# Linear attention and a SiLU block on one core: batch 1's exps of q placed further apart, PSUM bank sets in a cycle of four, and a third of one cast moved to GpSimd

## The chip, the cores and the metric

One core of a Trainium2 chip. The metric is the device time of one execution in microseconds (us). The kernel was already tuned; the question is what one more rearrangement of its first 45 us does to the time. Some words used below: PSUM is the memory that TensorE writes its products to; the kernel uses it as eight banks, and a bank is drained when the other engines have read it, so that TensorE may write it again. A transfer is issued when an engine starts it, and lands when its data are there.

## The reference

```python
# q, k, v: 8 batches, 8 heads, 576 positions, 64 columns, float32
q_s = exp(q - max(q)) / sum(...)          # softmax along the 64 columns
k_s = exp(k - max(k)) / sum(...)          # softmax along the 576 positions
kv  = einsum('bhsd,bhde->...', k_s, v)    # 64 x 64 per head
x   = einsum('bhsd,bhde->bhse', q_s, kv)  # 4608 rows of 512 after reordering
h   = x @ w_in                            # 512 -> 2048
out = (h * sigmoid(h)) @ w_out            # 2048 -> 512, float32
```

## The kernel before

The rows run in chunks. Only the opening matters here: batch 0's attention, the first product (w_in) of its 576 rows in 16 column blocks, the second product (w_out), and, between them, batch 1's attention. The start of the opening, with cuts:

```python
WIDE = (4, 0, 2, 6) * 3 + (4, 2, 0, 6)      # first PSUM bank of each of the 16 column blocks

def wide_mm(fb, cs):                        # first product, column block fb, parts cs of the 512 rows of w_in
    for n in range(2):
        for c in cs:
            nc.tensor.matmul(out=PS[:, WIDE[fb] + n, 0:S // 2], ...)

# the queue of loads on GpSimd, in this order
load_w1(0, 4, 0, 2); load_w1(0, 4, 2, 4)    # w_in, first quarter, in two halves
load_w1(4, 8); load_w1(8, 12); load_w1(12, 16)
load(1, "qt", q, 0, nc.gpsimd); load(1, "qt", q, 1, nc.gpsimd)      # q of batch 1
load_w2(0, 4)                               # w_out, first quarter
load(1, "kt", k, 0, nc.gpsimd); load(1, "kt", k, 1, nc.gpsimd)
load_w2(4, 8)
load(1, "vt", v, 0, nc.gpsimd); load(1, "vt", v, 1, nc.gpsimd)      # v of batch 1
...
vcast(0, 1, nc.scalar, 0, 1)                # v of batch 0, second cast: half each
vcast(0, 1, nc.vector, 1, 2)
...
wide_mm(0, (0, 1)); wide_mm(1, (0, 1)); wide_mm(2, (0, 1))          # needs the first half of w_in's first quarter alone
...
def wide(fb):                               # a unit for each column block
    wide_mm(fb, range(2 if fb < 3 else 0, NC))
    wide_silu(fb)                           # tanh on ScalarE, product on VectorE: this frees the banks
...
# placed before unit n; units 0 to 15 are the column blocks, b1 = 16 is the second product's first
plan(9,  lambda: (load_w2(8, 12), exp_q(1, 0, 0, 1)))
plan(10, lambda: (exp_q(1, 0, 1, 2), qsum_pair(1, 0)))              # GpSimd adds halves and quarters
plan(12, lambda: (exp_q(1, 1, 0, 1), qsum_end(1, 0)))
plan(13, lambda: (exp_q(1, 1, 1, 2), qsum_pair(1, 1), qnorm(1, 0, nc.gpsimd)))
plan(b1, lambda: (qsum_end(1, 1), qnorm(1, 1, nc.vector)))
plan(b1 + 6, lambda: ws_op(4, 1))           # a sum of w_in blocks, on VectorE
plan(b1 + 7, lambda: kv_both(1))            # kv product of batch 1, then its copy on VectorE
plan(b1 + 8, lambda: xt(1, 0))              # first product with that kv matrix
```

The softmax here doesn't subtract the row's maximum and nothing guards it: scores larger than these inputs give would overflow.

Of the kernel before, what the change touches and what calls it, by code (L numbers as in the profile page):

```python
# [17 lines left out]
def kernel(  # L18
# [9 lines left out]
    nc = tc.nc  # L28
    B, H, S, D = q.shape
# [3 lines left out]
    J = S // P  # L33
    NG = H // 2
    NC = DM // 128
# [31 lines left out]
    vaug = glob.tile([128, J, NG, E1], BF16, name="vaug")  # L67
# [19 lines left out]
    def copy(eng, o, i):  # L87
        if eng is nc.scalar:
            eng.copy(out=o, in_=i)  # L89
        else:  # L90
            eng.tensor_copy(o, i)  # L91

    def load(b, name, src, cc, eng):
        t = ld.tile([128, 2, J * D], FP32, name=name)
        st[b][name, cc] = t
        x = src[b].rearrange("(g r) (p j) d -> g (r p) (j d)", r=2, j=J)
        eng.dma_start(out=t, in_=x.rearrange("g x y -> x g y")[:, 2 * cc:2 * cc + 2, :])

    def jgd(b, name, cc):
        return st[b][name, cc].rearrange("p g (j d) -> p j g d", d=D)  # L100

    def half(t, cc):
        return t[:, :, cc * 128:(cc + 1) * 128].rearrange("p j (g d) -> p j g d", d=D)

    def exp_q(b, cc, g0=0, g1=2):
        if "eq" not in st[b]:
            st[b]["eq"] = ap.tile([128, J, NG * D], BF16, name="eq")
        nc.scalar.activation(  # L108
            out=half(st[b]["eq"], cc)[:, :, g0:g1], in_=jgd(b, "qt", cc)[:, :, g0:g1], func=ACT.Exp
        )  # L110

    def exp_k(b, cc):
        nc.scalar.activation(out=half(ek, cc), in_=jgd(b, "kt", cc), func=ACT.Exp)  # L113

    def vcast(b, cc, eng, g0=0, g1=2):
        o = vaug[:, :, 2 * cc + g0:2 * cc + g1, 0:D]
        i = jgd(b, "vt", cc)[:, :, g0:g1, :]
        copy(eng, o, i)

    def vcast_at(t, b, cc):  # L120

        if t == 2 and cc == 1:
            nc.gpsimd.tensor_copy(gate, SS[2][0:1, 0, 0:1])
        vcast(b, cc, nc.gpsimd)

    def qsum_pair(b, cc):
        e = half(st[b]["eq"], cc)
        t1 = mp.tile([128, 2 * TCH], FP32, name="h0", bufs=1)[:, 0:J * D]
        t1 = t1.rearrange("p (j g d) -> p j g d", g=2, d=D // 2)
        t2 = mp.tile([128, 2 * TCH], FP32, name=f"h{cc + 1}", bufs=1)[:, 0:J * D // 2]  # L130
        t2 = t2.rearrange("p (j g d) -> p j g d", g=2, d=D // 4)
        nc.gpsimd.tensor_tensor(
            out=t1, in0=e[:, :, :, 0:D // 2], in1=e[:, :, :, D // 2:D], op=ALU.add
        )
        nc.gpsimd.tensor_tensor(
            out=t2, in0=t1[:, :, :, 0:D // 4], in1=t1[:, :, :, D // 4:D // 2], op=ALU.add
        )
        st[b]["t2", cc] = t2

    def qsum_end(b, cc):  # L140
        new_zq(b)
        nc.vector.reduce_sum(out=st[b]["zq"][:, cc], in_=st[b]["t2", cc], axis=AX.X)
        nc.vector.reciprocal(out=st[b]["rzq"][:, cc], in_=st[b]["zq"][:, cc])

    def new_zq(b):
        if "zq" not in st[b]:
            st[b]["zq"] = ap.tile([128, 2, J, 2], FP32, name="zq", bufs=2)
            st[b]["rzq"] = ap.tile([128, 2, J, 2], FP32, name="rzq", bufs=2)

    def qsum(b, cc, gs=None):  # L150
        new_zq(b)
        z, e = st[b]["zq"][:, cc], half(st[b]["eq"], cc)
        if gs is None:
            nc.vector.reduce_sum(out=z, in_=e, axis=AX.X)  # L154
        else:
            nc.vector.reduce_sum(out=z[:, :, gs], in_=e[:, :, gs, :], axis=AX.X)
        if gs != 0:
            nc.vector.reciprocal(out=st[b]["rzq"][:, cc], in_=z)  # L158

    def qnorm(b, cc, eng):  # L160
        e = half(st[b]["eq"], cc)
        r = st[b]["rzq"][:, cc]
        eng.tensor_tensor(  # L163
            out=e, in0=e, in1=r[:, :, :, None].to_broadcast([128, J, 2, D]), op=ALU.mult
        )
# [21 lines left out]
    def trcopy(b, cc, j0, j1, bank, eng=nc.vector):  # L187
        t = PS[:, bank, :].bitcast(BF16)[:, 0:(j1 - j0) * 128].rearrange("x (j y) -> x j y", y=128)
        copy(eng, new_qt(b)[:, j0:j1, cc, :], t)
# [50 lines left out]
    def xt_evac(t, cc, bank, d0, d1, o0, eng):  # L240
        o = XTS[t % 2][:, 2 * cc:2 * cc + 2, o0:o0 + d1 - d0]
        copy(eng, o, PS[:, bank:bank + 2, d0:d1])
# [8 lines left out]
    def silu(t, fb, i, o, w):  # L251
        sg = mp.tile([128, S], FP32, name="sg", bufs=3)
        s = sg[:, 0:w]
        if len(i.shape) == 3:
            s = s.rearrange("p (a n) -> p a n", a=2)
        nc.scalar.activation(out=s, in_=i, func=ACT.Tanh, scale=OS)
        nc.vector.scalar_tensor_tensor(  # L257
            out=o, in0=s, scalar=1.0, in1=i, op0=ALU.add, op1=ALU.mult
        )


    WIDE = (4, 0, 2, 6) * 3 + (4, 2, 0, 6)

    def wide_mm(fb, cs):
        for n in range(2):
            for c in cs:
                nc.tensor.matmul(  # L267
                    out=PS[:, WIDE[fb] + n, 0:S // 2],
                    lhsT=W1[:, c, fb * 128:(fb + 1) * 128],
                    rhs=XTS[0][:, c, n * (S // 2):(n + 1) * (S // 2)],  # L270
                    start=(c == 0),
                    stop=(c == NC - 1),
                )

    def wide_silu(fb):
        bank = WIDE[fb]
        silu(
            0, fb, PS[:, bank:bank + 2, 0:S // 2],
            GTS[0][:, fb, :].rearrange("p (a n) -> p a n", a=2), S,
        )  # L280
# [268 lines left out]
    def heat(n, bank=5):  # L549
        for _ in range(n):  # L550
            nc.tensor.matmul(out=PS[:, bank, :], lhsT=warm[:, 0:128], rhs=warm, start=True, stop=True)

    def load_w1(f0, f1, c0=0, c1=NC):
        nc.gpsimd.dma_start(
            out=W1[:, c0:c1, f0 * 128:f1 * 128],
            in_=w_in[c0 * 128:c1 * 128, f0 * 128:f1 * 128].rearrange("(c p) f -> p c f", p=128),
        )

    def load_w2(f0, f1):
        nc.gpsimd.dma_start(  # L560
            out=W2[:, f0:f1, :],
            in_=w_out[f0 * 128:f1 * 128, :].rearrange("(fc p) o -> p fc o", p=128),
        )
# [8 lines left out]
    load_w1(4, 8)  # L572
    load_w1(8, 12)
    load_w1(12, 16)
    load(1, "qt", q, 0, nc.gpsimd)
    load(1, "qt", q, 1, nc.gpsimd)
    load_w2(0, 4)
# [11 lines left out]
    heat(7)  # L589
    qnorm(0, 1, nc.vector)  # L590
    vcast(0, 0, nc.scalar)
    trcopy(0, 0, 0, 5, 0, nc.scalar)
    trcopy(0, 0, 5, J, 1)
# [5 lines left out]
    xt_mm(0, 0, 0, 320, 4, 0)  # L599
    xt_mm(0, 0, 320, 256, 0, 0)  # L600
    heat(3, 6)
    vcast(0, 1, nc.scalar, 0, 1)
    vcast(0, 1, nc.vector, 1, 2)
    trcopy(0, 1, 0, 5, 2, nc.scalar)
    trcopy(0, 1, 5, J, 3)
    kv(0, 1)
# [6 lines left out]
    wide_mm(0, (0, 1))  # L613
    xt_evac(0, 1, 6, 0, 320, 0, nc.scalar)
    xt_evac(0, 1, 2, 0, 256, 320, nc.vector)
    wide_mm(1, (0, 1))
    wide_mm(2, (0, 1))


# [3 lines left out]
    def plan(u, f):  # L623
        at.setdefault(u, []).append(f)

    def wide(fb):
        wide_mm(fb, range(2 if fb < 3 else 0, NC))
        wide_silu(fb)

    for fb in range(NFB):  # L630
        units.append(lambda fb=fb: wide(fb))
# [138 lines left out]

    b1 = begin[1]

    plan(9, lambda: (load_w2(8, 12), exp_q(1, 0, 0, 1)))
    plan(10, lambda: (exp_q(1, 0, 1, 2), qsum_pair(1, 0)))
    plan(12, lambda: (exp_q(1, 1, 0, 1), qsum_end(1, 0)))
    plan(13, lambda: (exp_q(1, 1, 1, 2), qsum_pair(1, 1), qnorm(1, 0, nc.gpsimd)))
    plan(14, lambda: (load(2, "qt", q, 0, nc.gpsimd), load(2, "qt", q, 1, nc.gpsimd)))
    plan(b1 + 2, lambda: (exp_k(1, 0), exp_k(1, 1)))
    plan(b1 + 4, lambda: (tr(1, 0, 0, 5, 6), tr(1, 0, 5, J, 7)))
    plan(b1 + 4, lambda: (trcopy(1, 0, 0, 5, 6, nc.scalar), trcopy(1, 0, 5, J, 7)))  # L780
    plan(b1, lambda: (qsum_end(1, 1), qnorm(1, 1, nc.vector)))
    plan(b1, lambda: load_w2(12, 16))
    plan(b1 + 8, lambda: nc.scalar.copy(out=GTS[1][:, :, 0:64], in_=GTS[0][:, :, TCH:S]))
    plan(b1 + 3, lambda: (load(2, "kt", k, 0, nc.gpsimd), load(2, "kt", k, 1, nc.gpsimd)))
# [76 lines left out]
```

## Time and profile before

| | before |
|---|---|
| median, lowest, highest of three runs | 261.32, 261.06, 261.46 us |
| profiled execution, span | 262.14 us, 260.3 us |
| TensorE, VectorE, ScalarE, GpSimd busy | 97%, 80%, 72%, 25% |
| TensorE's one long idle time between 15 and 45 us | 0.78 us at 28.2 |

The prediction shows the lines of this profile that the forecast rests on.

```profile
24.30 0.65 ACT L256 ACTIVATE sg<-PS 128x576 f32<-128x576 f32 x1 [0.33 <-PE PS L267]
25.79 0.68 ACT L108 ACTIVATE eq<-qt 128x576 bf16<-128x576 f32 x1 [0.84 <-DMA qt<-in_q_dram]
26.38 0.63 ACT L256 ACTIVATE sg<-PS 128x576 f32<-128x576 f32 x1
26.91 0.67 ACT L108 ACTIVATE eq<-qt 128x576 bf16<-128x576 f32 x1
27.48 1.18 ACT L256 ACTIVATE sg<-PS 128x576 f32<-128x576 f32 x2
```

The tanh of block 9 had its input at 25.28, but the exp in front of it in ScalarE's order waited until q landed at 25.77. A size is given to the bank wait of TensorE at 28.96 in two ways: 0.78 us is idle time after the matmul before, and 0.95 us is how much later than due the held matmul started (matmuls in a row start 0.1225 us apart).

### The profile page before, as it was taken

To read this page: it belongs to the slowest core of one execution; us is meant where nothing else is said; L and a number is where in the kernel's file an instruction comes from. 1 tells how busy PE (TensorE), PEld (TensorE's weight loads), DVE (VectorE), ACT (ScalarE), POOL (GpSimd) and SP (SyncE) were. 2 spreads that over 40 slices of the span, in tenths; PEclk is the share of its full clock that TensorE was granted. 3 is DMA by queue.
4 is the path that set the end of the run, shared out by engine and by line. 5 is a ranking of instruction groups with operands and counts; after the bars stand their busy time and mean duration, and the time that the engine had idled before them with its cause. 6 is when DMAs were issued, how large, how long until landed. Compare 5 with 4: busy or idle time off the path is not lost.

```text
span 260.3 us, 6411 instructions
## 1 busy us (share of the span) xinstructions
PE 251.3 (97%) x2732; PEld 203.4 (78%) x2732; DVE 208.0 (80%) x268; ACT 187.5 (72%) x212; POOL 65.8 (25%) x63
## 2 busy tenths in 40 slices
PE   8799899999999999999999999999999999999992
PEld 3467656656888888888888888888888888888881
DVE  2867797998997999799979997999798548855932
ACT  5765978998993899489948995799573848484610
POOL 1743791650460306030603060306000000000003
PEclk9999999999999999999999999999999999999999
DMA  6999999679999585956694869530433003300624
GB/s 247 335 196 297 302 320 330 260 159 393 271 343 230 140 246 191 232 128 170 268 249 112 229 216 213 139 83 3 91 81 83 3 0 82 81 3 1 140 64 121
DMA packets 35964, 45.89 MB, mean 176 GB/s; under 512 B 16208, under 2 KB 21008, under 8 KB 35936
## 3 DMA queue, kind: packets, MB, share of 16 engines
q1 hardware_dynamic: 29568, 33.69, 47.5%
q0 software_dynamic: 6128, 11.60, 17.3%
q8 instruction: 21, 0.34, 0.6%
q10 hardware_dynamic: 240, 0.20, 0.2%
q14 instruction: 7, 0.06, 0.1%
HBM read 36.70 MB, written 9.44 MB: 177 GB/s over the span
## 4 chain that ended last, share of the span: by engine, by line
PE 66%; DVE 3%; POOL 1%; issue 0%; ACT 0%; POOLq 0%; DVEq 0%; ACTq 0%
PE PS L477 34%; PE PS L377 30%; PE PS L234 2%; DVE h L355 1%; PE PS L195 1%; DVE GT L451 1%; POOL out_dram L740 1%; DVE zq L154 0%; DVE ow L725 0%; ACT sc L493 0%; DVE ow L497 0%; DVE rzq L158 0%; POOLq L856 0%; DVE kvn L208 0%; DVE rz L206 0%
## 5 line engine op out<-in xcount | busy, mean ns | idle before, releaser
L355 DVE TENSOR_TENSOR h<-PS,h 128x1024 f32<-128x1024 f32 (+1 forms) x45 | 54.0, 1199 | 12.7 <-ACT h L89 6.3
L477 PEld LDWEIGHTS <-GT 128*128 128x128 f16 x512 | 49.6, 98 | 6.9 <-issue 1.2
L377 PEld LDWEIGHTS <-WS 128*128 128x128 f16 x480 | 46.8, 98 | 6.2 <-issue 0.5
L477 PE MATMUL PS<-W,GT 128*128 128x256 f16 x384 | 49.1, 273 | 0.0
L377 PE MATMUL PS<-XS,WS 128*128 128x256 f16 (+1 forms) x360 | 46.3, 272 | 0.1
L361 ACT ACTIVATE GT<-h 128x1024 f16<-128x1024 f32 (+1 forms) x45 | 46.1, 1047 | 0.1
L89 ACT COPY h<-PS 128x1024 f32<-128x1024 f32 (+1 forms) x35 | 35.1, 1003 | 13.1 <-PE PS L377 12.6
L163 POOL TENSOR_TENSOR eq<-eq,rzq 128x1152 bf16<-128x1152 bf16 x13 | 27.7, 2133 | 53.7 <-DVE rzq L158 53.3
L477 PEld LDWEIGHTS <-S 128*128 128x128 f16 x384 | 37.2, 98 | 5.2 <-issue 1.0
L377 PEld LDWEIGHTS <-W 128*128 128x128 f16 x360 | 34.7, 98 | 4.7 <-issue 0.2
L477 PE MATMUL PS<-T,S 128*128 128x256 f16 x256 | 32.7, 273 | 0.0
L377 PE MATMUL PS<-XT,W 128*128 128x256 f16 (+1 forms) x240 | 29.5, 272 | 0.0
L361 ACT ACTIVATE GT<-PS 128x1024 f16<-128x1024 f32 (+1 forms) x15 | 15.2, 1016 | 18.9 <-PE PS L377 18.9
L91 POOL CAST vaug<-vt 128x1152 bf16<-128x1152 f32 x12 | 14.8, 1240 | 44.4 <-DMA vt<-in_v_dram 36.0
L108 ACT ACTIVATE eq<-qt 128x1152 bf16<-128x1152 f32 (+1 forms) x18 | 19.1, 1059 | 3.3 <-DMA qt<-in_q_dram 3.2
L740 POOL DMA_DIRECT2D out_dram<-ow x5 | 2.7, 547 | 72.3 <-DVE ow L725 72.3
L113 ACT ACTIVATE ek<-kt 128x1152 bf16<-128x1152 f32 x16 | 18.4, 1153 | 1.4 <-DMA kt<-in_k_dram 1.4
L154 DVE TENSOR_REDUCE zq<-eq 128x18 f32<-128x1152 bf16 x12 | 16.1, 1345 | 3.8 <-ACT eq L108 3.8
L267 PE MATMUL PS<-XT,W 128*128 128x288 f16 x128 | 16.2, 286 | 0.8 <-DVE GT L257 0.8
L477 PE MATMUL PS<-W,S 128*128 128x256 f16 x128 | 16.5, 273 | 0.0
L497 DVE SCALAR_TENSOR_TENSOR ow<-PS,sc 128x512 f32<-128x512 f32 x7 | 4.8, 692 | 14.4 <-ACT sc L493 14.4
L267 PEld LDWEIGHTS <-W 128*128 128x128 f16 x128 | 12.4, 98 | 4.6 <-issue 1.2
(79 smaller groups left out, 346.7 us busy)
## 6 DMA issues: line engine op xcount, KB each, us to landing
out_dram<-ow SPq DMA_DIRECT2D x64, 128.0 KB, 2.4
qt<-in_q_dram SPq DMA_DIRECT2D x12, 576.0 KB, 4.7
kt<-in_k_dram SPq DMA_DIRECT2D x12, 576.0 KB, 5.6
vt<-in_v_dram SPq DMA_DIRECT2D x12, 576.0 KB, 5.4
qt<-in_q_dram POOLq DMA_DIRECT2D x4, 576.0 KB, 10.8
kt<-in_k_dram POOLq DMA_DIRECT2D x4, 576.0 KB, 13.8
vt<-in_v_dram POOLq DMA_DIRECT2D x4, 576.0 KB, 12.9
W<-in_moe_w_out_dram POOLq DMA_DIRECT2D x4, 512.0 KB, 15.2
```

The source lines that it names most:

```text
L89: eng.copy(out=o, in_=i)
L91: eng.tensor_copy(o, i)
L108: nc.scalar.activation(out=half(st[b]["eq"], cc)[:, :, g0:g1], in_=jgd(b, "qt", cc)[:, :, g0:g1], func=ACT.Exp)
L113: nc.scalar.activation(out=half(ek, cc), in_=jgd(b, "kt", cc), func=ACT.Exp)
L154: nc.vector.reduce_sum(out=z, in_=e, axis=AX.X)
L163: eng.tensor_tensor(out=e, in0=e, in1=r[:, :, :, None].to_broadcast([128, J, 2, D]), op=ALU.mult)
L267: nc.tensor.matmul(out=PS[:, WIDE[fb] + n, 0:S // 2], lhsT=W1[:, c, fb * 128:(fb + 1) * 128], rhs=XTS[0][:, c, n * (S // 2):(n + 1) * (S / ...
L355: nc.vector.tensor_tensor(out=four(t, i), in0=group_bank(t, True), in1=four(t, i), op=ALU.add)
L361: nc.scalar.activation(out=group_out(t, f, n), in_=x, func=ACT.Silu, scale=1.0 / XS)
L377: nc.tensor.matmul(out=PS[:, bank + p // 2, (p % 2) * HT:(p % 2) * HT + width(t)], lhsT=a[:, c, p * 128:(p + 1) * 128], rhs=bb[:, c, 0:wid ...
L477: nc.tensor.matmul(out=PS[:, bank, m * HN:(m + 1) * HN], lhsT=a[:, fc, m * 128:(m + 1) * 128], rhs=bb[:, fc, :], start=(first and fc == 0) ...
L740: eng.dma_start(out=rows(last, th * HT + a * 128 + i * P)[:, n * HN:(n + 1) * HN], in_=o[i * P:(i + 1) * P, :],)
```

## The change

Intent: place the exps of batch 1's q one at a time between tanhs, so that no bank is drained late; give every column block the bank set of the block four back (before, block 13 took that of block 10); and shorten batch 0's second cast of v by a third on GpSimd. GpSimd's additions for the second half of q's sums go, and VectorE sums that half itself.

```diff
+    def vcast(b, cc, eng, g0=0, g1=2, j0=0, j1=J):        # part of the rows
...
-    WIDE = (4, 0, 2, 6) * 3 + (4, 2, 0, 6)
+    WIDE = (4, 2, 0, 6) * 4
...
     load_w1(12, 16)
+    vcast(0, 1, nc.gpsimd, 0, 2, 6, J)
     load(1, "qt", q, 0, nc.gpsimd)
...
-    vcast(0, 1, nc.scalar, 0, 1)
-    vcast(0, 1, nc.vector, 1, 2)
+    vcast(0, 1, nc.scalar, 0, 1, 0, 6)
+    vcast(0, 1, nc.vector, 1, 2, 0, 6)
...
-    wide_mm(1, (0, 1))
     wide_mm(2, (0, 1))
...
-        wide_mm(fb, range(2 if fb < 3 else 0, NC))
+        wide_mm(fb, range(2 if fb in (0, 2) else 0, NC))
...
-    plan(9, lambda: (load_w2(8, 12), exp_q(1, 0, 0, 1)))
-    plan(10, lambda: (exp_q(1, 0, 1, 2), qsum_pair(1, 0)))
-    plan(12, lambda: (exp_q(1, 1, 0, 1), qsum_end(1, 0)))
-    plan(13, lambda: (exp_q(1, 1, 1, 2), qsum_pair(1, 1), qnorm(1, 0, nc.gpsimd)))
-    plan(14, lambda: (load(2, "qt", q, 0, nc.gpsimd), load(2, "qt", q, 1, nc.gpsimd)))
+    plan(9, lambda: load_w2(8, 12))
+    plan(10, lambda: exp_q(1, 0, 0, 1))
+    plan(11, lambda: (exp_q(1, 0, 1, 2), qsum_pair(1, 0)))
+    plan(14, lambda: (exp_q(1, 1, 0, 1), qsum_end(1, 0), qnorm(1, 0, nc.gpsimd)))
+    plan(15, lambda: qsum(1, 1, 0))
...
-    plan(b1, lambda: (qsum_end(1, 1), qnorm(1, 1, nc.vector)))
+    plan(b1, lambda: (exp_q(1, 1, 1, 2), qsum(1, 1, 1), qnorm(1, 1, nc.vector)))
+    plan(b1, lambda: (load(2, "qt", q, 0, nc.gpsimd), load(2, "qt", q, 1, nc.gpsimd)))
```

More of the change, by code (lines that the diff above doesn't have):

```diff
@@ L113, in exp_k @@
         nc.scalar.activation(out=half(ek, cc), in_=jgd(b, "kt", cc), func=ACT.Exp)
-    def vcast(b, cc, eng, g0=0, g1=2):
-        o = vaug[:, :, 2 * cc + g0:2 * cc + g1, 0:D]
-        i = jgd(b, "vt", cc)[:, :, g0:g1, :]
+    def vcast(b, cc, eng, g0=0, g1=2, j0=0, j1=J):
+        o = vaug[:, j0:j1, 2 * cc + g0:2 * cc + g1, 0:D]
+        i = jgd(b, "vt", cc)[:, j0:j1, g0:g1, :]
         copy(eng, o, i)
```

## The prediction

> **What bounds the kernel now.** I read the page's busy times and slices first, then the times of stretches, then the timeline of the first 45 us (the change touches nothing later), last the issues of single transfers with their time to landing. Page, busy row and slices of 6.5 us:
>
> ```profile
> PE 251.3 (97%) x2732; PEld 203.4 (78%) x2732; DVE 208.0 (80%) x268; ACT 187.5 (72%) x212; POOL 65.8 (25%) x63
> ...
> PE   8799899999999999999999999999999999999992
> ...
> DMA  6999999679999585956694869530433003300624
> ```
>
> TensorE is full, but so are the DMA engines in the first slices. The stretches (window and length, busy PE, PEld, DVE, ACT, POOL, clock, DMA share, GB/s):
>
> ```profile
> 15.00:19.20 4.20, 4.17 (x41) 3.06 (x33) 2.21 (x4) 2.43 (x5) 1.25 (x2) 1.00 1.23 205
> 19.20:28.20 9.00, 8.98 (x72) 7.04 (x73) 6.04 (x10) 6.31 (x11) 3.49 (x5) 1.00 1.17 290
> 28.20:29.00 0.80, 0.04 (x1) 0.04 (x1) 0.80 (x2) 0.80 (x2) 0.75 (x1) 1.00 1.03 373
> 29.00:32.00 3.00, 3.00 (x25) 2.37 (x25) 2.68 (x6) 2.54 (x5) 2.23 (x3) 1.00 1.12 310
> 32.00:39.07 7.07, 7.07 (x47) 3.58 (x45) 6.67 (x11) 5.41 (x7) 7.05 (x8) 1.00 1.14 314
> ```
>
> See the 0.8 us hole in TensorE at 28.2, and a DMA share above 1 in every row: the loads run back to back whatever TensorE does. The timeline (start, length, engine, instruction, idle before it and who ended that):
>
> ```profile
> 15.06 13.12 PE L267 MATMUL PS<-XT,W 128*128 128x288 f16 x104
> ...
> 19.18 8.81 PEld L267 LDWEIGHTS <-W 128*128 128x128 f16 x73 [0.34 <-DMA W<-in_moe_w_in_dram]
> ...
> 28.96 3.10 PE L267 MATMUL PS<-XT,W 128*128 128x288 f16 x24 [0.78 <-DVE GT L257]
> ...
> 31.94 3.61 PE L414 MATMUL PS<-W,GT 128*128 128x512 f16 x16
> ...
> 37.25 1.89 PE L414 MATMUL PS<-W,GT 128*128 128x512 f16 x8
> ...
> 38.28 0.68 ACT L89 CAST vaug<-vt 128x576 bf16<-128x576 f32 x1 [0.30 <-DMA vt<-in_v_dram]
> 38.28 0.76 DVE L91 CAST vaug<-vt 128x576 bf16<-128x576 f32 x1
> ...
> 39.07 0.69 PEld L195 LDWEIGHTS <-ek 64*64 64x64 bf16 x72 [0.42 <-ACT vaug L89]
> 39.07 0.81 PE L195 MATMUL PS<-vaug,ek 64*64 64x65 bf16 x72
> ```
>
> TensorE is held three times. At 19.18 the second quarter of w_in has only just landed. At 28.96 it waits for a PSUM bank that VectorE has not drained; this is the wait that the change aims at. At 39.07 the kv product of batch 1 waits for v's second cast, which both engines began when the transfer landed. Two issues of transfers with KB and us to landing:
>
> ```profile
> 24.93 0.72 POOL L97 DMA_DIRECT2D vt<-in_v_dram  x1 [2.26 <-DVE GT L257]
> ...
> vt<-in_v_dram POOLq DMA_DIRECT2D x1, 576.0 KB, 13.3
> W<-in_moe_w_out_dram POOLq DMA_DIRECT2D x1, 512.0 KB, 15.8
> ```
>
> v's last half is issued at 24.93 and lands 13.3 us later, at 38.2: it stands in a queue. The second row was issued at 19.43 (rows 4 to 7 of w_out's 16 blocks) and lands at 35.2. In the same way the first quarter of w_in lands at 14.2 and 16.05 (two halves), its second quarter at 19.14, its third at 21.7, its last at 24.3, q of batch 1 at 25.77 and 27.2, the first w_out quarter at 29.9, k at 31.4 and 32.9, v's first half at 36.8, the third w_out quarter at 40.7.
>
> **What the Trainium skill says.** "DMA: Bandwidth & Descriptors", section "Issuing engines are not separate DMA queues": all issues end on the same 16 DMA engines, and where one issues from saves only issue time. The trace agrees: landings follow each other by 1.47 us for 589,824 bytes, 401 GB/s, just under the 436 GB/s of its section "Where 436 GB/s comes from". "SBUF — State Buffer", section "Who interferes with whom": a VectorE instruction with two SBUF inputs contends with a GpSimd instruction that reads SBUF. The trace agrees: VectorE's normalisation of q took 1.36 us alone and 1.71 us where it overlapped GpSimd's at 34.2. "Perfetto Trace Analysis", section "Identifying Dependency Chains", has one look up the semaphores waited on; the issued order shows that the kv product now also waits for GpSimd at its 25th matmul.
>
> **The change, part by part.** *Banks.* Before, column block 13 of the first product takes the bank set of block 10, three blocks back; after, every block takes that of four back. Two matmuls cost 2 x 0.1225 us of spacing, a block of eight 0.98 us. A block's set is free some 1.65 us after its matmuls (block 4: ready 20.17, tanh at 20.38, VectorE's product 21.06 to 21.82), so three blocks of 0.98 between leave 1.29 us for delays. The delay before was two exps of 0.68 us in a row with tanhs: block 10's product ran at 28.15 to 28.91, and block 13 started at 28.96 in place of 28.01. That is 0.95 us, and it goes: with exps after tanh 9, 10, 13 and 15 I get the product of block 9 done at 26.7 (needed 28.0), of 10 at 27.8 (needed 29.0), of 11 at 28.9 (needed 30.0).
>
> *The early part.* The cast of 576 elements takes 0.68 us on ScalarE and 0.76 on VectorE; from 1152 in 1.17 and 576 in 0.68 a ScalarE element costs 0.85 ns, so 384 cost 0.16 us less, and VectorE at 1.04 ns 0.20 less. GpSimd's part is 384 elements; its casts of 1152 take 1.24 us, and with the 0.2 us of its one-element copy as a floor, 0.55 us. It starts at 12.83, is done at 13.4, and is read at the 25th of 36 matmuls, near 13.6. The product moves from 13.53 to 13.33, the first column block from 15.06 to 14.87. But then eight matmuls in place of twelve are done before w_in's second half is needed: at 15.85, and it lands at 16.05. Blocks 0 to 3 then end at 16.09 + 24 x 0.1225 = 19.03, and the second quarter lands at 19.14. Block 4 starts at 19.19, as before. The early part gives nothing.
>
> *After block 4.* 96 matmuls at 0.1225 end at 30.95, so the second product starts there in place of 31.94: 0.98 us ahead (0.95 and some spacing). Sixteen of its matmuls at 0.215 reach 34.39; nine transposes (0.5) 34.9; the next block needs w_out's second quarter, landed at 35.27: 0.4 us lost. 0.86 of matmuls to 36.2, transposes 36.7, eight matmuls to 38.4. Then kv waits for v: landed 38.26, cast by 39.04, start 39.07. The last 0.65 us are lost there. Sum of what reaches the end: 0.98 - 0.4 - 0.6 = 0, with at most 0.1 left (TensorE idled 0.09 us before kv in the kernel before).
>
> *Sums of q.* The second half's two GpSimd additions (1.29 and 0.80 us) and VectorE's short reduce (0.45) become two reduces of 0.744 on VectorE. By the order of instructions I get the normalisation's start at 34.29 against 34.23, without GpSimd's beside it, so 0.3 us shorter. VectorE must be free for v's cast at 38.26; before it was at 38.2, now near 37.9 to 38.2. No delay, but little slack.
>
> *GpSimd's queue.* The cast puts about 1 us into the issues of q, w_out and k: 12.34 becomes 13.3. They land 12 to 16 us after their issue, behind w_in, so no landing moves. q of batch 2 is issued earlier (33.5 for 34.67) and also stands in the queue.
>
> **Rivals.** First, the bank wait is on the path to the end and its 0.98 us are kept: 260.35 us. For it: TensorE is 97% busy and its order is unchanged. Against: kv's cast began 0.02 us after a landing, and landings do not depend on TensorE. It would need v to land earlier. Second, a new wait: VectorE late for v's cast by the added 1.04 us of reduces, or GpSimd's cast late and holding the first kv product, or issues late enough to empty the queue: 0.2 to 0.5 us more, 261.6. Against: slack of 0.25 us before w_in's half, 10 us of backlog in the queue. Third, TensorE's earlier work shifts later stages by freeing engines: ScalarE and VectorE work after 39 us hangs on kv, so it moves with it; at most 0.2 us either way.
>
> **Range and chances.** From the gate at 39.07 on, the two programs are the same instructions with the same inputs. I predict 261.2 us: 261.32 less 0.1 at most. The three runs spread over 0.4 us; the first rival gives the low end, 260.5 with part of it kept, the second the high end, 261.7. Two per cent is 5.2 us, over five times the largest effect found: within 0.98, faster 0.01, slower 0.01.
>
> **What would show it.** Right: the 0.78 us wait for VectorE gone and the second product starting near 31.0; block 4 still near 19.2 after a wait for w_in; new waits of about 0.4 us for w_out near 34.9 and 0.6 us for v's cast before kv; kv at 39.0 to 39.1. Wrong: kv before 38.7 (v landed earlier), or after 39.3 with VectorE busy at 38.3 (the reduces are on the path), or equal to before up to 45 us and different later.

## The result, and the profile after

| | before | after |
|---|---|---|
| median, lowest, highest of four runs | 261.39, 261.06, 261.50 us | 261.56, 261.29, 261.79 us |
| ratio, 95% interval | | 1.0008 (0.9991 to 1.0026) |
| profiled execution, span | 262.14, 260.3 us | 261.29, 259.5 us |

A ratio compares the fast runs of the two kernels in the same rounds, so it is not quite the ratio of the medians. The kernel is not shown to be faster or slower: the interval holds 1, and 261.56 us lies in the forecast range (260.5 to 261.7).

The two *profiles*, on the other hand, differ by 0.8 us of span in favour of the changed kernel. That is a trap: the profile of before caught an execution slower than its four timed ones, the profile after the fastest of its four. The page's busy row and the stretches of the changed kernel (columns as in the prediction):

```profile
PE 251.4 (97%) x2732; PEld 203.6 (78%) x2732; DVE 208.2 (80%) x269; ACT 187.5 (72%) x212; POOL 64.3 (25%) x62
```

```profile
28.20:29.00 0.80, 0.80 (x9) 0.63 (x7) 0.80 (x2) 0.50 (x1) 0.71 (x2) 1.00 1.05 365
29.00:32.00 3.00, 3.00 (x22) 2.01 (x21) 2.74 (x6) 2.77 (x5) 1.42 (x2) 1.00 1.09 344
32.00:39.07 7.07, 7.07 (x116) 3.98 (x114) 6.97 (x12) 5.61 (x8) 5.89 (x8) 1.00 1.16 301
```

The hole at 28.2 is filled (0.80 of 0.80 us), and the loads still run back to back. The timeline of the changed kernel:

```profile
13.05 0.51 ACT L89 CAST vaug<-vt 128x384 bf16<-128x384 f32 x1 [0.16 <-DMA vt<-in_v_dram]
13.05 0.36 DVE L91 CAST vaug<-vt 128x384 bf16<-128x384 f32 x1 [0.65 <-DMA vt<-in_v_dram]
13.09 0.70 POOL L91 CAST vaug<-vt 128x384 bf16<-128x384 f32 x1 [0.48 <-DMA vt<-in_v_dram]
...
15.10 15.85 PE L267 MATMUL PS<-XT,W 128*128 128x288 f16 x128
...
30.79 3.62 PE L414 MATMUL PS<-W,GT 128*128 128x512 f16 x16
...
37.59 0.75 DVE L91 CAST vaug<-vt 128x576 bf16<-128x576 f32 x1
...
37.93 0.83 PEld L195 LDWEIGHTS <-ek 64*64 64x64 bf16 x72 [0.42 <-issue]
37.93 0.94 PE L195 MATMUL PS<-vaug,ek 64*64 64x65 bf16 x72
...
39.94 0.38 PE L234 MATMUL PS<-qT,kvn 64*64 64x448 bf16 x4
```

All 128 matmuls of the first product run in one piece and the second product starts at 30.79 in place of 31.94: 1.15 us earlier. At the first product with batch 1's kv matrix (39.94 for 40.78) the lead is 0.84 us. And in this execution the loads came early: v's last half landed at 37.56, not 38.26. How much of the 0.84 us is the change and how much the landings can't be read from two profiles. It takes more profiles, and a table of what each stage waits for.

### The profile page after: what moved, and what is told of

It reads as the page before. It is cut to its first block, busy times and chain, and to the rows that moved or that the text cites. A ratio compares the mean times of both kernels' runs of the same rounds, so it can differ in the third digit from the quotient of the medians.

```text
span 259.5 us, 6411 instructions
## 1 busy us (share of the span) xinstructions
PE 251.4 (97%) x2732; PEld 203.6 (78%) x2732; DVE 208.2 (80%) x269; ACT 187.5 (72%) x212; POOL 64.3 (25%) x62
## 4 chain that ended last, share of the span: by engine, by line
PE 66%; DVE 4%; POOL 1%; issue 0%; ACT 0%; POOLq 0%; DVEq 0%; ACTq 0%
PE PS L477 34%; PE PS L377 30%; PE PS L234 2%; DVE h L355 1%; PE PS L195 1%; DVE GT L451 1%; POOL out_dram L740 1%; DVE zq L154 0%; DVE ow L725 0%; ACT sc L493 0%; DVE ow L497 0%; DVE rzq L158 0%; POOLq L857 0%; DVE kvn L208 0%; DVE rz L206 0%
## 5 line engine op out<-in xcount | busy, mean ns | idle before, releaser
L377 PEld LDWEIGHTS <-W 128*128 128x128 f16 x360 | 34.7, 98 | 4.7 <-issue 0.2
L91 POOL CAST vaug<-vt 128x1152 bf16<-128x1152 f32 (+1 forms) x13 | 15.5, 1197 | 45.5 <-DMA vt<-in_v_dram 35.2
L451 DVE TENSOR_TENSOR GT<-GT 128x2048 f16<-128x2048 f16 x8 | 15.7, 1968 | 0.0
```

Source lines behind the costliest of these rows:

```text
L91: eng.tensor_copy(o, i)
L377: nc.tensor.matmul(out=PS[:, bank + p // 2, (p % 2) * HT:(p % 2) * HT + width(t)], lhsT=a[:, c, p * 128:(p + 1) * 128], rhs=bb[:, c, 0:wid ...
L451: nc.vector.tensor_tensor(out=o[:, f], in0=in0[:, f], in1=in1[:, f], op=op)
```

## The experiments

All are timed in five rounds beside the kernel before, and each gave one profile. The runs came in three groups of four, in the order given here, each group on a chip of its own, so part of what differs between profiles of different groups may be the chip. "Landing" is the start of a transfer's issue plus its time to landing.

### The kernel before and the changed kernel, once more (no edit)

> The unchanged kernel as its own control, with a second profile. Theory A (prediction: the landings set the start of batch 1's kv product and do not vary): landings as in the first profile within 0.1 us (v's last half at 38.2, q at 25.77), bank wait 0.95 us, ratio 1.000 with an interval of at most 0.002 either way. Theory B (landings vary from execution to execution, and the first profile of this kernel caught a late one: its execution took 262.14 us against a median of 261.39): here q lands 0.3 to 0.5 us earlier, near 25.3 to 25.5, the bank wait shrinks below 0.6 us, and the span is near 259.6 us.

> The changed kernel once more. Theory A: ratio 0.999 to 1.001, no bank wait. Theory B: the same ratio, 0.998 to 1.001, but its landings of v differ from those of the first profile of it (37.56) by 0.2 us or more, and the span follows the landing nearly one for one.

Measured: before again 261.86 us median, ratio 1.0005 (0.9987 to 1.0023), span 260.1; v's last half landed at 37.96, q at 25.75, bank wait 0.92 us. Changed again 261.78 us, 1.0009 (0.9988 to 1.0030), span 260.5; v landed at 38.38. Theory A is wrong that landings repeat: of one and the same kernel they moved by 0.3 us (before) and 0.8 us (changed). Whether that is the execution or the chip can't be told apart: the record does not say on which chip the first two profiles were taken. Theory B is right that they move, and wrong that q would land much earlier here, so that the bank wait stayed. The span of the changed kernel grew by 1.0 us where v's landing grew by 0.82. A slow piece of the second profile of the changed kernel, TensorE's timeline:

```profile
15.29 1.15 PE L267 MATMUL PS<-XT,W 128*128 128x288 f16 x8
16.98 14.87 PE L267 MATMUL PS<-XT,W 128*128 128x288 f16 x120 [0.54 <-DMA W<-in_moe_w_in_dram]
31.69 3.62 PE L414 MATMUL PS<-W,GT 128*128 128x512 f16 x16
```

This is a wait that the kernel before never showed: after eight matmuls TensorE needs the second half of w_in's first quarter, which landed at 16.94 here.

### The banks alone

```diff
-    WIDE = (4, 0, 2, 6) * 3 + (4, 2, 0, 6)
+    WIDE = (4, 2, 0, 6) * 4
-    wide_mm(1, (0, 1))
-        wide_mm(fb, range(2 if fb < 3 else 0, NC))
+        wide_mm(fb, range(2 if fb in (0, 2) else 0, NC))
```

> The changed cycle of bank sets and order of the first column blocks alone, exps and casts as before. Theory A: the bank wait is gone (block 13 now waits for block 9, whose product is done by 28), time 0.998 to 1.001 of before. If the bank wait is really on the path to the end, as the first rival has it: 0.996 to 0.997.

Measured: 261.53 us, ratio 1.0001 (0.9981 to 1.0020). The wait did not go, it moved to the first matmul of the second product, which needs banks that the last column blocks used:

```profile
31.74 3.61 PE L414 MATMUL PS<-W,GT 128*128 128x512 f16 x16 [0.69 <-DVE GT L257]
```

The second product starts 12.61 us after block 4, against 12.75 and 12.71 in the kernel before and 11.76 in the changed one. So the bank cycle alone gives nearly nothing: with the exps in their old places the drains run late as a row, and the cycle only chooses where TensorE meets them. My expectation that the cycle takes the wait away was wrong. The other half, the exps in their new places on the old cycle, was not run, so that both parts are needed is not shown.

### The changed kernel without GpSimd's third of the cast

```diff
-    vcast(0, 1, nc.gpsimd, 0, 2, 6, J)
-    vcast(0, 1, nc.scalar, 0, 1, 0, 6)
-    vcast(0, 1, nc.vector, 1, 2, 0, 6)
+    vcast(0, 1, nc.scalar, 0, 1)
+    vcast(0, 1, nc.vector, 1, 2)
```

> The changed kernel without GpSimd's third of the cast. Theory A: no difference from the changed kernel (0.999 to 1.001 of it), since the early part is gated by the landing of w_in. If GpSimd's cast costs something (its later issues of transfers, or its cast holding the kv product): faster than the changed kernel by 0.2 to 0.5 us, ratio to before 0.997 to 0.999.

Measured: 261.29 us, ratio 0.9991 (0.9968 to 1.0015): no difference that the noise lets through. In the profile the first column block starts 2.29 us after the landing of batch 0's v without GpSimd's part, and 2.07 us with it in both profiles of the changed kernel; so the part can save 0.2 us there, as forecast. (In the edited kernels that keep it, it was 2.06 to 2.44 us; what holds the upper ones was not looked into.) Its profiled execution (262.99 us, the slowest of six) had one transfer of q take 3.2 us in place of 1.47, and every later landing with it.

### Batch 1 without its own k (wrong result): v lands early

```diff
-    load(1, "kt", k, 0, nc.gpsimd)
-    load(1, "kt", k, 1, nc.gpsimd)
+    for i in range(2):
+        st[1]["kt", i] = st[0]["kt", i]
```

> Wrong result on purpose: in the kernel before, batch 1 takes batch 0's k, so 1.18 MB less stand in the queue and v's last half lands about 2.9 us earlier, near 35.1. Gate theory (time is the later of TensorE's own chain and v's landing plus some 2.4 us): this kernel is held by its bank wait of 0.9 us and by TensorE, so the early landing gives it nothing: ratio 0.999 to 1.000, batch 1's first product with the kv matrix at 40.6 to 40.8 as before. If the landing held this kernel as well: 0.995 to 0.998.

> Wrong result on purpose: the changed kernel with batch 0's k in batch 1, v landing near 35.1. Gate theory: the gain of the removed bank wait now reaches the end, 0.9 to 1.1 us: ratio 0.995 to 0.997, first product with the kv matrix near 39.6 to 39.8. Rival (the gain is lost later whatever v does, for instance to ScalarE or VectorE): ratio 0.999 to 1.001.

Measured: before 261.33 us, 0.9990 (0.9968 to 1.0011), first product with the kv matrix at 40.29; changed 261.14 us, 0.9982 (0.9959 to 1.0006), at 40.73. (The comparison with the reference still passed, here and for q below: with these inputs the other batch's data seem to change the result by less than its bound.) The kernel before reached that product earlier than forecast: q landed earlier too, at 25.21, and the bank wait was 0.46 us. For the changed kernel the timed runs don't decide between the theories, since the interval reaches into both forecasts; the profile does. The first product with the kv matrix came 0.9 us later than the gate theory had it, although v landed at 36.32. Two things make that up. The second half of w_in's first quarter landed late (16.83), so that block 4 started at 19.82 and the second product at 31.58, some 0.6 us later than forecast. The other 0.31 us are VectorE. Timeline of the kernel before without k:

```profile
39.52 0.18 DVE L206 RECIPROCAL rz<-PS 128x4 f32<-128x4 f32 x1 [0.28 <-PE PS L195]
```

and of the changed kernel without k:

```profile
38.39 0.75 DVE L91 CAST vaug<-vt 128x576 bf16<-128x576 f32 x1
...
39.05 0.41 DVE L91 COPY qT<-PS 128x512 bf16<-128x512 bf16 x1
39.38 0.68 DVE L328 TENSOR_TENSOR WS<-W,WS 128x1024 f16<-128x1024 f16 x1
39.98 0.17 DVE L206 RECIPROCAL rz<-PS 128x4 f32<-128x4 f32 x1
```

In the kernel before VectorE waits 0.28 us for the kv product; in the changed one it comes to v's cast 2 us after the landing and then runs without a gap. The time from the second product's start to the first product with the kv matrix is 8.84 us in every profile of the kernel before without a late v (three, and one of the banks alone), and 9.15, 9.16 and 9.15 us in three of the changed kernel: VectorE takes back 0.31 us.

### v of batch 1 one place later in the queue

```diff
-    load(1, "vt", v, 0, nc.gpsimd)
-    load(1, "vt", v, 1, nc.gpsimd)
...
-    plan(9, lambda: (load_w2(8, 12), exp_q(1, 0, 0, 1)))
+    plan(9, lambda: (load_w2(8, 12), load(1, "vt", v, 0, nc.gpsimd),
+                     load(1, "vt", v, 1, nc.gpsimd), exp_q(1, 0, 0, 1)))   # likewise in the changed kernel
```

> The kernel before with v of batch 1 queued behind the third quarter of w_out, so it lands about 2.4 us later, near 40.6 (correct result). Gate theory: first product with the kv matrix at 43.0 to 43.2, 2.2 to 2.4 us later, ratio 1.007 to 1.010. If v's landing sets nothing: 0.999 to 1.001.

> The changed kernel with the same late v. Gate theory: the same time as the kernel before with late v within 0.2 us, although it has no bank wait: ratio 1.007 to 1.010. If the bank wait's 0.95 us count beside the landing: 1.004 to 1.006.

Measured: before 264.36 us, 1.0108 (1.0069 to 1.0147); changed 265.11 us, 1.0120 (1.0094 to 1.0146). That v's landing sets the time is shown: in the changed kernel the forecast for a bank wait that counts beside the landing (1.004 to 1.006) lies outside the interval. With v late, the kernel without the bank wait is not shown to be any faster than the one with it. That they agree within 0.2 us is not shown: their medians differ by 0.75 us, and both lost somewhat more than the gate theory forecast. Timeline of the kernel before with late v:

```profile
40.84 0.48 PE L195 MATMUL PS<-vaug,ek 64*64 64x65 bf16 x36 [1.14 <-ACT vaug L89]
...
41.14 0.76 DVE L91 CAST vaug<-vt 128x576 bf16<-128x576 f32 x1 [2.37 <-DMA vt<-in_v_dram]
...
41.86 0.57 PE L195 MATMUL PS<-vaug,ek 64*64 64x65 bf16 x36 [0.54 <-ACT vaug L89]
...
43.48 0.38 PE L234 MATMUL PS<-qT,kvn 64*64 64x448 bf16 x4
```

v landed at 41.11; the first product with the kv matrix follows 2.37 us later (cast, copy, sum, reciprocal and kv copy one after another on VectorE). The same 2.4 us stand between v's landing and that product in the first profile of the changed kernel (37.56, 39.94) and in the one without GpSimd's cast (39.39, 41.77). In the changed kernel's profile with late v it took 3.29 us, since TensorE's granted clock fell to half for three microseconds (column before the last two):

```profile
41.20:42.20 1.00, 1.00 (x37) 0.71 (x37) 1.00 (x3) 1.00 (x2) 0.49 (x1) 0.50 1.10 323
```

### The changed kernel with one VectorE sum moved behind the kv copy

```diff
-    plan(b1 + 6, lambda: ws_op(4, 1))
-    plan(b1 + 8, lambda: t_op(1, nc.vector))
+    plan(b1 + 8, lambda: (ws_op(4, 1), t_op(1, nc.vector)))
```

> The changed kernel with one sum of w_in blocks (0.68 us of VectorE) moved behind the kv matrix of batch 1. VectorE theory: in the changed kernel VectorE's chain from the normalisation of q to the kv matrix is 0.31 us longer than TensorE's own work, so the first product with the kv matrix starts 9.15 us after the second product's start in place of 8.84; here it is back at 8.84 to 8.90, or at v's landing plus 2.2 us if that is later. If v's landing alone makes the 0.31 us: still 9.1 or more. Time 0.1 to 0.3 us less than the changed kernel, inside the noise.

Measured: 261.54 us, 0.9988 (0.9969 to 1.0007); the time from the second product to the first product with the kv matrix is 8.99 us, 0.16 of the 0.31 us back:

```profile
38.85 0.18 DVE L206 RECIPROCAL rz<-PS 128x4 f32<-128x4 f32 x1 [0.32 <-PE PS L195]
...
39.63 0.38 PE L234 MATMUL PS<-qT,kvn 64*64 64x448 bf16 x4
```

VectorE waits for TensorE again at the reciprocal. The rest fits v's cast, which started at 37.45 while v had landed at 37.18, since the sums ahead of it still hold VectorE: the kv product, whose second half needs that cast, took 0.94 us where it takes 0.81 in the kernel before. So the VectorE theory is right in kind, and my figure of 8.84 to 8.90 a little too good.

### The changed kernel with twelve early matmuls

```diff
     wide_mm(2, (0, 1))
+    wide_mm(1, (0, 1))
-        wide_mm(fb, range(2 if fb in (0, 2) else 0, NC))
+        wide_mm(fb, range(2 if fb < 3 else 0, NC))
```

> The changed kernel with column block 1's first matmuls back among the early ones (twelve, not eight, before the second half of w_in's first quarter is needed), on the changed cycle of banks. Order theory: block 4 starts at the latest of 3.93 us after block 0, 2.5 us after that half's landing, and 0.05 us after the second quarter's landing; in the changed kernel it was 2.99 us after the half, 0.33 behind the second quarter, so here at most 0.1 us behind the second quarter where the landings are late. If the order is without effect: block 4 still 0.3 us behind the second quarter and 2.99 behind the half.

Measured: 262.17 us, 1.0009 (0.9988 to 1.0029). The half of w_in landed at 17.51, later than in any other profile, and still block 4 started 2.58 us after it and 0.05 us after its own quarter. With eight early matmuls it started 2.99 to 3.00 us after that half in four profiles where this half was late (the second one of the changed kernel, and those without GpSimd's cast, without k and with late v), 0.32 to 0.34 us behind its quarter. So the new order cost 0.3 us in each of the four profiles where the half was late. v landed at 38.84 and the first product with the kv matrix followed 2.37 us later, so the 0.3 us were not to be seen at the end.

### Both edits on the changed kernel

```diff
-    plan(b1 + 6, lambda: ws_op(4, 1))
-    plan(b1 + 8, lambda: t_op(1, nc.vector))
+    plan(b1 + 8, lambda: (ws_op(4, 1), t_op(1, nc.vector)))
     wide_mm(2, (0, 1))
+    wide_mm(1, (0, 1))
-        wide_mm(fb, range(2 if fb in (0, 2) else 0, NC))
+        wide_mm(fb, range(2 if fb < 3 else 0, NC))
```

> The changed kernel with both of these edits, the candidate that should beat both kernels: no bank wait, block 4 within 0.1 us of the second quarter's landing when that is late, first product with the kv matrix 8.84 to 9.0 us after the second product's start. By the terms 0.3 to 0.6 us less than the changed kernel: ratio to before 0.9975 to 0.9995. If execution to execution differences of the landings swamp it: 0.999 to 1.001.

Measured: 261.47 us, 0.9990 (0.9971 to 1.0009). Block 4 started 0.05 us behind its quarter (19.41 and 19.36), the second product 11.77 us after it, the first product with the kv matrix 9.20 us later: 2.21 us after v's landing at 38.17, and TensorE waiting for v. Each term does what it should, and yet the version is not shown to beat the kernel before: its interval holds 1. It was not timed in the same rounds as the changed kernel.

### The kernel before, batch 1 without its own q (wrong result)

```diff
-    load(1, "qt", q, 0, nc.gpsimd)
-    load(1, "qt", q, 1, nc.gpsimd)
+    for i in range(2):
+        st[1]["qt", i] = st[0]["qt", i]
```

> Wrong result on purpose: in the kernel before, batch 1 takes batch 0's q, so its exps wait for no landing. Landing theory of the bank wait (it has been the time from block 4's start to q's landing, less 5.63 us, in four profiles): wait below 0.1 us, second product 11.8 us after block 4's start, ratio 0.996 to 0.998 (all later landings are 2.9 us earlier too). If the two exps in a row make the wait, whatever q does: 0.4 us or more remain.

Measured: 260.87 us, ratio 0.9965 (0.9949 to 0.9981), the only one clear of noise in the good direction, by 0.9 us. TensorE's timeline, with the old banks and the old places of the exps:

```profile
15.63 15.85 PE L267 MATMUL PS<-XT,W 128*128 128x288 f16 x128
31.34 3.61 PE L414 MATMUL PS<-W,GT 128*128 128x512 f16 x16
```

No bank wait, and the first exp starts at 25.21, right behind a tanh. Two exps in a row are no cause by themselves; the cause was q's landing, with the tanhs standing behind the exp that waited for it. It follows that placing the first exp one block later, without the new cycle, might have been enough; that was not run. The gain of 0.9 us belongs to both things that this edit does: the wait goes, and v lands early as well (35.37), so that nothing takes the lead back. In the profiles of the kernel before the wait was the time from block 4's start to q's landing less 5.63 us: 6.58, 6.54, 6.08 and 6.52 us gave waits of 0.94, 0.92, 0.46 and 0.89 us.

### All profiles in one table

Times from the span's start; "kv use" is the first product with batch 1's kv matrix.

| profile | block 4 | second product | difference | v landed | kv use | after second product | after v |
|---|---|---|---|---|---|---|---|
| before | 19.19 | 31.94 | 12.75 | 38.26 | 40.78 | 8.84 | 2.52 |
| before again | 19.21 | 31.92 | 12.71 | 37.96 | 40.76 | 8.84 | 2.80 |
| banks alone | 19.13 | 31.74 | 12.61 | 37.77 | 40.58 | 8.84 | 2.81 |
| before, no k | 19.13 | 31.45 | 12.32 | 34.60 | 40.29 | 8.84 | 5.69 |
| before, no q | 19.56 | 31.34 | 11.78 | 35.37 | 40.19 | 8.85 | 4.82 |
| before, late v | 19.81 | 32.50 | 12.69 | 41.11 | 43.48 | 10.98 | 2.37 |
| changed | 19.03 | 30.79 | 11.76 | 37.56 | 39.94 | 9.15 | 2.38 |
| changed again | 19.93 | 31.69 | 11.76 | 38.38 | 40.85 | 9.16 | 2.47 |
| changed, no GpSimd cast | 19.70 | 31.46 | 11.76 | 39.39 | 41.77 | 10.31 | 2.38 |
| changed, no k | 19.82 | 31.58 | 11.76 | 36.32 | 40.73 | 9.15 | 4.41 |
| changed, late v (half the clock) | 19.33 | 31.09 | 11.76 | 40.38 | 43.67 | 12.58 | 3.29 |
| changed, sum moved | 18.88 | 30.64 | 11.76 | 37.18 | 39.63 | 8.99 | 2.45 |
| changed, twelve early | 20.09 | 31.86 | 11.77 | 38.84 | 41.21 | 9.35 | 2.37 |
| changed, both | 19.41 | 31.18 | 11.77 | 38.17 | 40.38 | 9.20 | 2.21 |

Kv use is the later of two times: the second product plus 8.84 us (9.15 in the changed kernel), or v's landing plus 2.37 us. That holds within 0.1 us in every row but three: with the sum moved the first distance is 8.99 us in place of 9.15, with both edits the second is 2.21 us, since the moved sum no longer stands there, and with half the clock it is 3.29 us.

From kv use to the start of the last matmul it is 214.0 to 214.6 us. These 0.6 us are no smaller than the effect looked for, and the two kernels don't share them evenly: the median is 214.0 us in the six profiles of the kernel before and its edits (the first six rows) and 214.2 in the eight of the changed one and its edits. TensorE starts its matmuls at the same distances from kv use, save in a few places. The one that differs in most profiles is a matmul near 79 us: it comes at the later of 38.5 us after kv use and 2.88 us after GpSimd has normalised the second half of batch 3's q. In four of the six it was held by less than 0.05 us, in the other two by about 0.25 and 0.3; in the eight changed ones by 0.07 to 0.63, most of them 0.2 to 0.3. Timeline of GpSimd, the kernel before again and the changed kernel again:

```profile
74.16 2.12 POOL L163 TENSOR_TENSOR eq<-eq,rzq 128x1152 bf16<-128x1152 bf16 x1 [1.12 <-DVE rzq L158]
```

```profile
74.65 2.12 POOL L163 TENSOR_TENSOR eq<-eq,rzq 128x1152 bf16<-128x1152 bf16 x1 [1.47 <-DVE rzq L158]
```

Kv use differs by 0.09 us between these two, this start by 0.49. Why GpSimd starts later there was not tested.

## Why the prediction was right or wrong

- **The time: right, in part by luck.** No change, inside the range; and that v's landing takes the lead back is right in kind. But the two losses that I summed to zero are not the ones that the runs show.
- **The bank wait goes: right**, with its size. In no profile of the changed kernel does TensorE wait for a bank in the first product, and the second product starts 11.76 us after block 4. But I gave two exps in a row as the cause; batch 1 without its own q showed that it is q's landing. So the wait is a transfer's too, 0.46 us in one profile (without k) and 0.95 in another.
- **The early part gives nothing: right in kind, undersized.** GpSimd's part moved the first column block 0.2 us nearer to the landing of batch 0's v, as worked out, although its casts missed: GpSimd took 0.70 us for 0.55, VectorE 0.36 for 0.56. The new wait for w_in's second half, which I had at 0.2 us and harmless, reached 0.5 us of idle time in the changed kernel's second profile and costs 0.3 us at block 4 when that half is late.
- **The losses after block 4: the step that failed.** I put 0.4 us on a wait for w_out's second quarter and 0.6 us on kv waiting for v's cast. Neither profile of the unedited changed kernel shows the first (w_out landed at 34.56, was used at 34.75), because landings and TensorE shift together; it came as 0.87 us in one profile, where a transfer was late, and as 0.1 us in the two with twelve early matmuls. The second was a misreading: the gap of 0.42 us before kv's weight load, laid to the cast, is there as well at 37.93 in the changed kernel, before that cast had ended (38.34), and only the second half of kv needs it. What takes the lead back is one step later, at kv use: 0.31 us to VectorE's longer chain, and what is left to v's landing plus 2.37 us.
- **Sums of q, "no delay, but little slack": wrong.** I compared VectorE with a fixed landing; the comparison that counts is with TensorE, which now comes 0.98 us sooner. VectorE's normalisation starts 3.26 us after the second product, against 2.29 before: the two reduces make up the difference, one of 0.74 us ahead of the last column block's product and one of 0.74 where 0.45 stood. It is 0.35 us shorter, as forecast, but 0.31 us of lateness are left at kv use. The line of the kernel before and that of the changed one:

```profile
34.23 1.71 DVE L163 TENSOR_TENSOR eq<-eq,rzq 128x1152 bf16<-128x1152 bf16 x1
```

```profile
34.05 1.36 DVE L163 TENSOR_TENSOR eq<-eq,rzq 128x1152 bf16<-128x1152 bf16 x1
```

- **GpSimd's queue, "no landing moves": wrong, since landings are not fixed.** Between two profiles of one kernel v's landing moved by 0.8 us, as much as the whole effect. That the later issues don't matter is not contradicted by any run, but against such shifts it is not shown either.

Sum, as an estimate with the landings of the two profiles of the kernel before put into the changed kernel's terms. First profile: the second product at 19.19 + 11.76 = 30.95; kv use at the later of 30.95 + 9.15 = 40.10 and 38.26 + 2.37 = 40.63, against 40.78: 0.15 us gained. Second profile: block 4 at 16.41 + 2.99 = 19.40, the second product at 31.16, kv use at the later of 40.31 and 40.33, against 40.76: 0.43 us gained. So of 0.95 us of removed wait 0.5 to 0.8 never reach the end. The measured difference lies between 0.3 us faster and 0.8 us slower (the interval of the second comparison); a gain of 0.15 fits, one of 0.43 lies just outside it. What comes after kv use closes that: in the second profiles it is 0.30 us longer in the changed kernel (214.29 for 213.99), which leaves 0.13 us, and in the first ones it is the same (214.2). That this later loss belongs to the change, and not to chance, is not shown. One hint is open too: the second half of w_in came 2.0 us or more after the first in five of eight profiles with the changed placement of exps and in none of six with the old one, although the programs differ there in little; that may be chance.

## What to carry to other kernels

A wait named after an engine can start with a transfer: look at what stands in front of the late instruction in its own engine's order, and ask what that waited for. Where loads run back to back, compare a removed wait with the next landing *and* with every other engine's distance to the faster stage, since an engine that was just in time becomes the bound when TensorE comes early. And take several profiles before reading a difference of less than one per cent from two of them: here the profiles differed by 0.8 us in one direction and the timed runs by 0.2 in the other.

## What the Trainium skill lacked or had wrong

- "VectorE: DVE Perf Modes", section "Mode 2×_2P — use both read ports for one tensor", has a condition that fits what VectorE's casts did, 0.36 us for six rows of 64 where nine rows took 0.755: an even outermost dimension. I had not looked it up and forecast 0.555. It also lets odd equal dimensions through; nine rows on both sides did not get it here. Whether the contiguous source counted as one row of 576, no run shows.
- "TensorE: Matmul & The Clock Gate", section "Part 1: The HAM clock gate (the "warmup" mystery)", lets the clock fall after an idle window of about 3.4 us, and does not say how much work a window may hold and still count as idle. In the changed kernel with late v, idle times of 1.79 and 0.60 us with 36 small matmuls between them were followed by half the clock for three microseconds; in the kernel before with late v, idle times of 1.14 and 0.54 us were not.
- No page that I read says how far landings move between executions of one program: 0.3 and 0.8 us between two profiles, for a transfer that lands near 38 us, and once 3.2 us for a transfer that mostly takes 1.47.
